# Key-value blocks of 32 by 32 in a linear-attention block, kept side by side and set onto the diagonal by ScalarE

## The chip, the core and the metric

The kernel runs on one core of a Trainium2 chip. The metric is device time in microseconds (us) of one execution. Before the change the median of three executions is 479.77 us (479.7 to 479.87). The engines are named as the profile names them: PE (TensorE), with PEld for its weight loads, DVE (VectorE), ACT (ScalarE), POOL (GpSimd) and SP (SyncE, which issues most loads).

## The reference

A transformer block with adaptive layer norm: linear attention with 32 heads of 16, then a dense Mish MLP. S is 2048, D is 512, F is 1792, and everything is fp32.

```python
def attention(h):                                  # A_ref
    q, k, v = qkv(h)                               # (1, 32, 2048, 16) each
    phi = lambda t: jnp.where(t > 0, t + 1, jnp.exp(t)) + 1e-6
    pq, pk = phi(q), phi(k)
    kv = jnp.einsum("bhsd,bhse->bhde", pk, v)      # one 16 x 16 block per head
    z = jnp.einsum("bhsd->bhd", pk)
    num = jnp.einsum("bhqd,bhde->bhqe", pq, kv)
    den = jnp.einsum("bhqd,bhd->bhq", pq, z)[..., None] + 1e-6
    return merge_heads(num / den) @ wo

sa, ca, ga, sb, cb, gb = split(silu(c) @ w_mod)    # six rows of 512
x = x + ga * attention(layernorm(x) * (1 + ca) + sa)
x = x + gb * mlp(layernorm(x) * (1 + cb) + sb)     # mlp: mish(h @ w1 + b1) @ w2
```

## The kernel before

The order of the instructions on each engine is the order in which the program is written. Pieces of side work are generators: `spawn` adds one, `spawn_idle` adds one of lower rank, and each `tick()` between two units of TensorE work takes one step of each running generator. All large SBUF tiles (128 x 512 fp32) come from one pool of 93 slots, `sb`; PSUM has four `acc`, three `h` and one `tp` bank.

Matmuls run in fp32r on halves: `split` writes a high half `...h` (ScalarE or POOL, line 82 or 84) and a low half `...l` (VectorE, line 88 or 90), and `mm3` (lines 72 to 76) issues high x high, low x high and high x low. A few small products run in plain fp32, among them the two of this case's centre: `den` (line 946, the denominators) and `kv_ps` (line 1176).

The stages in order of time, in the profiled execution:

- To about 116 us: layer norm of x in four blocks of 512 rows (each four row tiles `x_0` to `x_3`), transposes (`tp_x`, line 279), keys (`pk`, `ku`), and the Gram product `gacc` of phi(k) with the normalised x. For the early tiles the sum and the square sum come from ScalarE; `sums_eps` (line 225, then a power on POOL, line 199) turns them into 1/std `rs_x`, `sums_shift` (line 229) makes `nb_x`, and ScalarE applies both (line 208). `make_constants` builds masks on POOL at about 30 to 33 us; `bmask` (128 x 128) is one on the 16 x 16 blocks of the diagonal.
- About 116 to 126 us: the queries of the first blocks (lines 74 to 76 and 417), then `den`, then `kv_ps`: for each group g of 128 columns, the 128 x 128 block of phi(k)^T v, of which only two 64 x 64 diagonal parts are computed (j = 0, 1), summed over four row tiles `zs[k]`, `wv[k]`. VectorE writes them, times `bmask`, into the zeroed tile `kv`; `kv` is split into `kvh` and `kvl`; at 134.5 us `m_ps` (lines 74 to 76) multiplies them with wo to give `m`.
- To about 190 us: more queries, the attention output `o` (line 1001, twelve matmuls for each row tile: four groups g by three terms), the second layer norm (`rs_n`, `nb_n`, ScalarE's `n`, VectorE's 32 x 32 transposes `wide_n<-n`, line 239).
- From 190 us: the MLP as a Strassen-like scheme of seven products over quarters of w1 and w2. Sums of w1's quarters (`s`, `a`) are split early by the generator `early_rows`; the first products use `b_0h`, `b_0l` (the second layer norm) against `a_0h`, `a_0l`.

`mod_side` loads chunks of w_mod (SP) and reduces each with silu(c) on VectorE (line 175) into a column of `mc`: chunks 12 to 15 (`sb`), 16 to 19 (`cb`) and 20 to 23 (`gb`). After chunk 23, `bcast_row` turns gb's four columns into a row (`gb_ps`, TensorE; `gb_row`, ScalarE; two DMAs, POOL).

Of the kernel before, what the change touches and what calls it, by code (L numbers as in the profile page):

```python
# [25 lines left out]
def block_kernel(ctx: ExitStack, tc: tile.TileContext, x, wqkv, wo, w1, b1t, w2, c, wmodt, out):  # L26
# [11 lines left out]
    def sb(name, dt=F32, shape=(P, 512)):  # L38

        return big.tile(list(shape), dt, tag="T", name=name, bufs=SLOTS)  # L40
# [4 lines left out]
    def f32(t):  # L45
        return t.bitcast(F32)
# [97 lines left out]
    ident = cst.tile([P, P], F32, name="ident")  # L144
    make_identity(nc, ident)
    w32 = cst.tile([P, P], F32R, name="w32")
    bmask = cst.tile([P, P], F32, name="bmask")
    hmask = cst.tile([P, 4, 32], F32, name="hmask")

    kv = sb("kv")  # L150

    def make_constants():
        pool.memset(f32(w32), 1.0 / 32)
        pool.memset(kv, 0.0)

        pool.memset(bmask, 1.0)
        bm3 = bmask.rearrange("p (a r) -> p a r", r=16)
        pool.affine_select(bm3, bm3, pattern=[[-16, 8], [0, 16]], compare_op=ALU.is_ge,
                           fill=0.0, base=0, channel_multiplier=1)
        pool.affine_select(bm3, bm3, pattern=[[16, 8], [0, 16]], compare_op=ALU.is_ge,  # L160
                           fill=0.0, base=15, channel_multiplier=-1)

        pool.memset(hmask, 1.0)
        pool.affine_select(hmask, hmask, pattern=[[128, 4], [-16, 32]], compare_op=ALU.is_ge,
                           fill=0.0, base=0, channel_multiplier=1)
        pool.affine_select(hmask, hmask, pattern=[[-128, 4], [16, 32]], compare_op=ALU.is_ge,
                           fill=0.0, base=15, channel_multiplier=-1)
# [56 lines left out]
    def sums_eps(key, b, t, sums):  # L224
        dve.tensor_scalar(rs[key, b][:, t:t + 1], sums[:, 1:2], 1.0 / D, EPS, op0=ALU.mult, op1=ALU.add)  # L225
        ln_rstd(key, b, t, t + 1)
# [453 lines left out]
    apply(1, 1, act, shift=False)  # L680
    step(kpost[2])
    sums_eps("x", 1, 2, sums2)
    step(xsplit[2], kpost[2], xsplit[3])
    g_unit(0, 1)
    sums_eps("x", 1, 3, sums3)
    sums_shift("x", 1, 2, sums2)
    apply(1, 2, act, shift=False)
    step(kpost[3])
# [305 lines left out]
    def o_unit(b, t, tag="acc"):  # L994
        seeded = (b, t) in seeds
        p = seeds.pop((b, t)) if seeded else ps(tag, f"o_{b}_{t}")
        ts = slice(P * t, P * (t + 1))
        for g in range(4):
            st, mv_ = [q[:, ts] for q in qs[b, g]], ms[g]
            for i, (l, r) in enumerate(((st[0], mv_[0]), (st[0], mv_[1]), (st[1], mv_[0]))):  # L1000
                pe.matmul(p, l, r, start=not seeded and g == 0 and i == 0, stop=g == 3 and i == 2,  # L1001
                          skip_group_check=seeded)
        spawn(o_post(p, b, t, seeded))

    def later_sums(b, t):
# [146 lines left out]
    def beside_q(n):  # L1152
        if n < 4:
            load_x(1, n, "r")
        else:
            load_x(2, n - 4, "r")
        if n == 1:
            spawn(kv_side())
            spawn(wo_scale())
        if n == 4:  # L1160
            spawn(mod_side([20, 21, 22, 23, 16, 17, 18, 19], 2))
        tick()
        if n == 6:
            next(early_rows[0])
# [3 lines left out]
    kvs = {}  # L1168
    attending = attend(0, 3)
    next(attending)  # L1170
    kv_ps = ps("acc", "kv_ps")
    for g in range(4):
        for k in range(4):
            for j in range(2):
                cs = slice(P * g + 64 * j, P * g + 64 * (j + 1))
                pe.matmul(kv_ps[64 * j:64 * (j + 1), cs], wv[k][:, cs], zs[k][:, cs], start=k == 0, stop=k == 3)
    run(early_rows[0])
    for j in range(2):
        js = slice(64 * j, 64 * (j + 1))
        dve.tensor_tensor(kv.rearrange("p (g m) -> p g m", g=4)[js, :, js],  # L1180
                          kv_ps.rearrange("p (g m) -> p g m", g=4)[js, :, js],
                          bmask[js, js].unsqueeze(1).to_broadcast([64, 4, 64]), op=ALU.mult)
    kv_halves = split("kv", kv, kvs, 0)
    next(kv_halves)
    next(attending)
    run(kv_halves)
    for g in range(4):
        q_unit(2, g)
        if g == 1:
            spawn(attending)  # L1190
        if g == 2:
            spawn(attend(1, 4))
        if g == 1:
            spawn(mod_side(range(12, 16), 1))
        load_x(3, g, "r")
        if g == 2:
            for k in range(4):
                m_ps = ps("acc", f"m_ps_{k}")
                mm3(m_ps, [h[:, P * k:P * (k + 1)] for h in kvs[0]], wos[k], True, True)
                spawn(split(f"m_{k}", m_ps, ms, k))  # L1200
        tick()
    for g in range(4):
        seed_next()
        q_unit(3, g)
        tick()
        if g == 1:
            spawn_idle(early_rows[1])
            for t in range(4):
                seed_next()
                o_unit(0, t)  # L1210
                spawn(norm_first(0, t))
                if t == 1:
                    spawn(attend(2, 5, sp))
                tick()
# [471 lines left out]
```

## Time and profile before

| | |
|---|---|
| median of three executions | 479.77 us (479.7 to 479.87) |
| the profiled execution | 480.13 us, of which the span on the engines is 478.4 |
| PE busy | 471.6 us (99%) |
| DVE busy | 391.4 us (82%) |
| ACT busy | 309.3 us (65%) |
| POOL busy | 138.0 us (29%) |
| granted TensorE clock | 1.0 |
| DMA | 85.44 MB, mean 179 GB/s |

A row of the timeline reads: start in us, duration in us, engine, line of the kernel, operation, output tile<-input tiles, partitions x elements, and how many of them were grouped; in brackets the idle time of the engine before it and what ended it. For matmuls the form is contraction rows * output rows, then the moving operand. Durations of PE overlap, since matmuls are pipelined: what one costs is read from start to start. A row of the waits names the engine and the line that waited, what it waited for, and the sum, the count and the longest in us. A row of windows gives the stretch, its length, and for PE, PEld, DVE, ACT and POOL the busy time and the number of instructions, then the granted clock.

### The profile page before, as it was taken

To read this page: it belongs to the slowest core of one execution; us is meant where nothing else is said; L and a number is where in the kernel's file an instruction comes from. 1 tells how busy PE (TensorE), PEld (TensorE's weight loads), DVE (VectorE), ACT (ScalarE), POOL (GpSimd) and SP (SyncE) were. 2 spreads that over 40 slices of the span, in tenths; PEclk is the share of its full clock that TensorE was granted. 3 is DMA by queue.
4 is the path that set the end of the run, shared out by engine and by line. 5 is a ranking of instruction groups with operands and counts; after the bars stand their busy time and mean duration, and the time that the engine had idled before them with its cause. 6 is when DMAs were issued, how large, how long until landed. Compare 5 with 4: busy or idle time off the path is not lost.

```text
span 478.4 us, 7106 instructions
## 1 busy us (share of the span) xinstructions
PE 471.6 (99%) x2290; PEld 388.2 (81%) x2290; DVE 391.4 (82%) x784; ACT 309.3 (65%) x556; POOL 138.0 (29%) x235
## 2 busy tenths in 40 slices
PE   7999999999999999999999999999999999999997
PEld 6778887878887888888888888888888888888887
DVE  6989897998999889698879864899444787779992
ACT  6977559757657976588778756594256676637700
POOL 3586261100023255012225325334011101354400
PEclk9999999999999999999999999999999999999999
DMA  8913649544674356927548669999643603497974
GB/s 296 355 53 79 121 103 277 146 158 132 203 226 134 107 129 180 322 89 222 176 128 242 226 176 290 383 319 261 204 104 88 129 5 88 111 219 159 243 157 104
DMA packets 81568, 85.44 MB, mean 179 GB/s; under 512 B 23505, under 2 KB 55769, under 8 KB 81530
## 3 DMA queue, kind: packets, MB, share of 16 engines
q1 hardware_dynamic: 55176, 47.08, 33.9%
q0 software_dynamic: 24096, 37.12, 29.4%
q10 hardware_dynamic: 2258, 0.79, 0.8%
q8 instruction: 18, 0.29, 0.2%
q14 instruction: 20, 0.16, 0.1%
HBM read 55.32 MB, written 22.81 MB: 163 GB/s over the span
## 4 chain that ended last, share of the span: by engine, by line
PE 82%; DVE 7%; DMA 4%; ACT 4%; POOL 2%; issue 1%; ACTq 0%
PE p_a L1254 15%; PE o L1001 9%; PE p_s L1254 8%; PE oacc L75 5%; PE oacc L74 5%; PE oacc L76 5%; PE m L75 5%; PE m L76 5%; PE m L74 5%; PE p L1254 4%; PE pq_a L417 2%; PE pq L74 2%; PE pq L76 2%; PE pq L75 2%; DMA wm<-in_wmodt_dram 1%; PE pk L319 1%
## 5 line engine op out<-in xcount | busy, mean ns | idle before, releaser
L1259 DVE TENSOR_TENSOR cb<-p_s,u 128x512 f32<-128x512 f32 x28 | 19.2, 687 | 12.3 <-ACT u L1307 10.7
L842 POOL DMA_DIRECT2D wb<-w2d x14 | 9.8, 704 | 65.1 <-PE m L76 28.2
L1246 ACT ACTIVATE ub<-cb,b1c 128x512 f32<-128x512 f32 x28 | 20.1, 720 | 9.2 <-DVE cb L1259 8.9
L199 POOL TENSOR_TENSOR rs_n<-rs_n,half 128x1 f32<-128x1 f32 x16 | 10.1, 630 | 39.1 <-DVE rs_n L225 18.9
L1582 POOL DMA_DIRECT2D wt_m<-w2t x20 | 14.0, 702 | 25.2 <-PE m L76 16.9
L1264 ACT ACTIVATE p<-p_a 128x512 f32<-128x512 f32 x12 | 7.0, 582 | 19.8 <-PE p_a L1254 11.7
L1307 ACT ACTIVATE u<-p_a 128x512 f32<-128x512 f32 x14 | 8.4, 598 | 13.8 <-PE p_a L1254 13.6
L1221 ACT ACTIVATE u<-p,b1c 128x512 f32<-128x512 f32 x14 | 9.6, 685 | 11.5 <-PE p L1254 11.5
L1221 ACT ACTIVATE u<-p_a,b1c 128x512 f32<-128x512 f32 x14 | 9.6, 686 | 8.5 <-PE p_a L1254 8.3
L313 POOL DMA_DIRECT2D ku<-ku x10 | 8.9, 1035 | 19.6 <-DVE ku L304 19.4
L848 POOL DMA_DIRECT2D w2b<-w2d x20 | 10.6, 542 | 12.9 <-PE oacc L76 7.6
L953 POOL DMA_DIRECT2D rden_d<-rden x2 | 1.5, 737 | 42.4 <-DVE rden L951 42.4
L270 ACT ACTIVATE hf_n<-sq_n,mc 128x512 f32<-128x512 f32 x16 | 12.0, 803 | 2.4 <-DMA w2r<-in_w_dram 2.4
L304 DVE SCALAR_TENSOR_TENSOR ku<-e_k,relu_k 128x512 f32<-128x512 f32 x16 | 11.0, 685 | 0.9 <-ACT relu_k L302 0.9
L304 DVE SCALAR_TENSOR_TENSOR q<-e_q,relu_q 128x512 f32<-128x512 f32 x16 | 10.7, 690 | 1.2 <-ACT relu_q L302 1.2
L199 POOL TENSOR_TENSOR rs_x<-rs_x,half 128x1 f32<-128x1 f32 (+1 forms) x10 | 7.8, 785 | 13.1 <-DVE rs_x L194 12.2
L190 DVE BATCH_NORM_STATS2 st_x<-x 128x6 f32<-128x512 f32 x13 | 8.8, 677 | 2.9 <-DMA x<-in_x_dram 2.9
L256 POOL DMA_DIRECT2D sq_n<-wide_n x16 | 8.7, 553 | 6.8 <-DVE wide_n L239 4.7
L175 DVE SCALAR_TENSOR_TENSOR wm<-wm,sc_row 128x512 f32<-128x512 f32 x16 | 10.5, 686 | 0.0
L965 DVE SCALAR_TENSOR_TENSOR q<-q,rd 128x512 f32<-128x512 f32 x16 | 10.4, 683 | 0.1
L256 POOL DMA_DIRECT2D sq_x<-wide_x x16 | 8.9, 566 | 5.1 <-DVE wide_x L239 4.6
L301 ACT ACTIVATE e_k<-pk 128x512 f32<-128x512 f32 x16 | 9.5, 591 | 0.9 <-PE pk L322 0.9
(1634 smaller groups left out, 1862.3 us busy)
## 6 DMA issues: line engine op xcount, KB each, us to landing
wm<-in_wmodt_dram SPq DMA_DIRECT2D x24, 256.0 KB
w1p<-in_w_dram SPq DMA_DIRECT2D x24, 256.0 KB
w2b<-w2d POOLq DMA_DIRECT2D x20, 256.0 KB, 6.6
wt_m<-w2t POOLq DMA_DIRECT2D x20, 256.0 KB, 3.6
r<-in_x_dram SPq DMA_DIRECT2D x16, 256.0 KB
x<-in_x_dram SPq DMA_DIRECT2D x15, 256.0 KB
w2r<-in_w_dram SPq DMA_DIRECT2D x14, 256.0 KB
wb<-w2d POOLq DMA_DIRECT2D x14, 256.0 KB, 3.4
```

The costliest lines, as they stand in the source:

```text
L74: pe.matmul(o, st[0], mv[0], start=start, stop=False)
L75: pe.matmul(o, st[0], mv[1], start=False, stop=False)
L76: pe.matmul(o, st[1], mv[0], start=False, stop=stop)
L199: pool.tensor_tensor(y, y, half[:, lo:hi], op=ALU.pow)
L256: queues[n % len(queues)].dma_start(v[32 * m:32 * (m + 1), :, a, :], w[32 * a:32 * (a + 1), m:16:4].rearrange("p j t c -> p j (t c)"))
L304: dve.scalar_tensor_tensor(dst, e, 1.0, r, op0=ALU.min, op1=ALU.add)
L1001: pe.matmul(p, l, r, start=not seeded and g == 0 and i == 0, stop=g == 3 and i == 2, skip_group_check=seeded)
L1221: act.activation(u, p, AF.Mish, bias=b1c[:, f:f + 1])
L1246: act.activation(u, p, AF.Mish, bias=b1c[:, f:f + 1])
L1254: pe.matmul(p, st, mv, start=onto is None and c == 0 and i == 0, stop=c == 1 and i == 2, skip_group_check=onto is not None)
L1259: dve.tensor_tensor(out, p, u, op=ALU.add)
L1582: pool.dma_start(v, w2t[g][:, :, SUM[name], :])
```

## The change

1. The key-value product computes 32 x 32 diagonal blocks (j = 0 to 3) instead of 64 x 64 ones, twice as many calls, each with half the stationary and half the moving columns. The blocks lie side by side in a 128 x 128 piece of PSUM.
2. The mask `kvmask` is 128 x 32, made by a VectorE reduction of `bmask` in `make_constants`. VectorE writes `kvc` (128 x 128), it is split into `kvch` and `kvcl`, and ScalarE sets each half onto the diagonal with four copies of 32 x 4 x 32 into two tiles `kv`, zeroed by POOL during the queries.
3. `early_rows[0]`, whose last part makes the low halves of w1's first quarters, runs from the tick of the second unit of the last queries instead of right behind the product.
4. `mod_side` takes chunks 16 to 19 and 12 to 15 first; 20 to 23 (gb) come one to a tick from the last queries on.
5. The attention output's twelve matmuls are ordered by terms (high x high for all four groups, then high x low, then low x high).
6. `sums_eps` of row tile 3 of block 1 stands one place earlier.

PE around the key-value product, before (`kv_ps` stands for the product, `zs` and `wv` are its operands, a row with x2 is two calls; the pattern goes on to sixteen such rows) and then after:

```order
L946 MATMUL den_1530<-q_1_1374,hmask 32x128 x4
L946 MATMUL den_1530<-q_2_1430,hmask 32x128 x4
L946 MATMUL den_1530<-q_3_1437,hmask 32x128 x4
L1176 MATMUL kv_ps<-zs_1353,wv_958 64x64 x2
L1176 MATMUL kv_ps<-zs_1355,wv_1000 64x64 x2
L1176 MATMUL kv_ps<-zs_1357,wv_1038 64x64 x2
L1176 MATMUL kv_ps<-zs_1359,wv_1061 64x64 x2
```

```order
L946 MATMUL den_1534<-q_1_1374,hmask 32x128 x4
L946 MATMUL den_1534<-q_2_1430,hmask 32x128 x4
L946 MATMUL den_1534<-q_3_1437,hmask 32x128 x4
L1179 MATMUL kv_ps<-zs_1353,wv_958 32x32 x4
L1179 MATMUL kv_ps<-zs_1355,wv_1000 32x32 x4
L1179 MATMUL kv_ps<-zs_1357,wv_1038 32x32 x4
L1179 MATMUL kv_ps<-zs_1359,wv_1061 32x32 x4
```

Each row has become four calls of 32 x 32 where it was two of 64 x 64; `den` ahead of it already has four calls of 32 rows.

VectorE (DVE) at about 26 to 33 us, before and then after. `rs_x<-sums_x_3` is the first half of 1/std of row tile 3, `nb_x<-sums_x_3` the step that needs POOL's power of it; `xn_`, `pk_` are halves for the Gram product, `st_x` the statistics of the next block:

```order
L304 SCALAR_TENSOR_TENSOR ku_2_342<-e_k_2_343,relu_k_2_344 128x512
L225 TENSOR_SCALAR rs_x_329<-sums_x_2_376 128x1
L88 TENSOR_TENSOR xn_2l<-x_2_72,xn_2h 128x512
L90 SCALAR_TENSOR_TENSOR pk_2l<-ku_2_342,pk_2h 128x512
L225 TENSOR_SCALAR rs_x_329<-sums_x_3_387 128x1
L229 TENSOR_TENSOR nb_x_330<-sums_x_2_376,rs_x_329 128x1
L304 SCALAR_TENSOR_TENSOR ku_3_347<-e_k_3_348,relu_k_3_349 128x512
L229 TENSOR_TENSOR nb_x_330<-sums_x_3_387,rs_x_329 128x1
L88 TENSOR_TENSOR xn_3l<-x_3_77,xn_3h 128x512
L90 SCALAR_TENSOR_TENSOR pk_3l<-ku_3_347,pk_3h 128x512
L190 BN_STATS st_x_0_466<-x_0_435 128x6
L191 BN_AGGR mv_x_463<-st_x_0_466 128x2
```

```order
L304 SCALAR_TENSOR_TENSOR ku_2_341<-e_k_2_342,relu_k_2_343 128x512
L225 TENSOR_SCALAR rs_x_328<-sums_x_2_375 128x1
L225 TENSOR_SCALAR rs_x_328<-sums_x_3_386 128x1
L88 TENSOR_TENSOR xn_2l<-x_2_72,xn_2h 128x512
L90 SCALAR_TENSOR_TENSOR pk_2l<-ku_2_341,pk_2h 128x512
L229 TENSOR_TENSOR nb_x_329<-sums_x_2_375,rs_x_328 128x1
L304 SCALAR_TENSOR_TENSOR ku_3_346<-e_k_3_347,relu_k_3_348 128x512
L229 TENSOR_TENSOR nb_x_329<-sums_x_3_386,rs_x_328 128x1
L88 TENSOR_TENSOR xn_3l<-x_3_77,xn_3h 128x512
L90 SCALAR_TENSOR_TENSOR pk_3l<-ku_3_346,pk_3h 128x512
L161 TENSOR_REDUCE kvmask<-bmask 128x32
L190 BN_STATS st_x_0_466<-x_0_435 128x6
```

`rs_x<-sums_x_3` moved ahead of `xn_2l` and `pk_2l`, and `kvmask` stands between `pk_3l` and the statistics.

VectorE at about 158 to 163 us, in the second layer norm of block 0, before and then after (`wm,mc` is one chunk of w_mod; `s_1` are sums of w1's quarters):

```order
L239 STREAM_TRANSPOSE wide_n_1989<-n_0_1954 128x16x32
L1024 SCALAR_TENSOR_TENSOR nb_n_1876<-osum_1_1908,rs_n_1875 128x1
L1021 TENSOR_SCALAR rs_n_1875<-osum_2_1971 128x1
L868 TENSOR_TENSOR s_1_2000<-w1p_1_1880 128x256
L869 TENSOR_TENSOR s_1_2000<-s_1_2000,w1p_0_1879 128x256
L870 TENSOR_TENSOR s_1_2001<-w1p_0_1879,w1p_1_1880 128x256
L871 TENSOR_TENSOR s_1_2001<-w1p_0_1879,s_1_2000 128x256
L239 STREAM_TRANSPOSE wide_n_1989<-n_1_1992 128x16x32
L1024 SCALAR_TENSOR_TENSOR nb_n_1876<-osum_2_1971,rs_n_1875 128x1
L1021 TENSOR_SCALAR rs_n_1875<-osum_3_1996 128x1
L239 STREAM_TRANSPOSE wide_n_1989<-n_2_2024 128x16x32
```

```order
L175 SCALAR_TENSOR_TENSOR wm_1890,mc<-wm_1890,sc_row 128x512
L239 STREAM_TRANSPOSE wide_n_2022<-n_0_1984 128x16x32
L1023 SCALAR_TENSOR_TENSOR nb_n_1895<-osum_1_1936,rs_n_1894 128x1
L1020 TENSOR_SCALAR rs_n_1894<-osum_2_2001 128x1
L868 TENSOR_TENSOR s_1_2033<-w1p_1_1907 128x256
L869 TENSOR_TENSOR s_1_2033<-s_1_2033,w1p_0_1906 128x256
L870 TENSOR_TENSOR s_1_2034<-w1p_0_1906,w1p_1_1907 128x256
L871 TENSOR_TENSOR s_1_2034<-w1p_0_1906,s_1_2033 128x256
L175 SCALAR_TENSOR_TENSOR wm_1932,mc<-wm_1932,sc_row 128x512
L239 STREAM_TRANSPOSE wide_n_2022<-n_1_2025 128x16x32
L1023 SCALAR_TENSOR_TENSOR nb_n_1895<-osum_2_2001,rs_n_1894 128x1
L1020 TENSOR_SCALAR rs_n_1894<-osum_3_2029 128x1
```

A product of w_mod now stands ahead of each `wide_n<-n`. The four products of w_mod that stood among `q`, `qs_2l` and `qs_3l` at about 146 to 152 us are gone from there; in their place, behind the last `q`, stand `a_0l`, `s_0l`, `s_0l`, `a_0l`, which were ahead of the key-value mask.

```diff
@@ -144,21 +144,21 @@
     ident = cst.tile([P, P], F32, name="ident")
     make_identity(nc, ident)
     w32 = cst.tile([P, P], F32R, name="w32")
-    bmask = cst.tile([P, P], F32, name="bmask")
     hmask = cst.tile([P, 4, 32], F32, name="hmask")
 
-    kv = sb("kv")
+    kvmask = cst.tile([P, 32], F32, name="kvmask")
+    kv = []
 
     def make_constants():
         pool.memset(f32(w32), 1.0 / 32)
-        pool.memset(kv, 0.0)
-
+        bmask = sb("bmask", F32, (P, P))
         pool.memset(bmask, 1.0)
         bm3 = bmask.rearrange("p (a r) -> p a r", r=16)
         pool.affine_select(bm3, bm3, pattern=[[-16, 8], [0, 16]], compare_op=ALU.is_ge,
                            fill=0.0, base=0, channel_multiplier=1)
         pool.affine_select(bm3, bm3, pattern=[[16, 8], [0, 16]], compare_op=ALU.is_ge,
                            fill=0.0, base=15, channel_multiplier=-1)
+        dve.tensor_reduce(kvmask, bmask.rearrange("p (a c) -> p c a", c=32), op=ALU.add, axis=mybir.AxisListType.X)
 
         pool.memset(hmask, 1.0)
         pool.affine_select(hmask, hmask, pattern=[[128, 4], [-16, 32]], compare_op=ALU.is_ge,
@@ -680,9 +680,9 @@
     apply(1, 1, act, shift=False)
     step(kpost[2])
     sums_eps("x", 1, 2, sums2)
+    sums_eps("x", 1, 3, sums3)
     step(xsplit[2], kpost[2], xsplit[3])
     g_unit(0, 1)
-    sums_eps("x", 1, 3, sums3)
     sums_shift("x", 1, 2, sums2)
     apply(1, 2, act, shift=False)
     step(kpost[3])
@@ -995,11 +995,10 @@
         seeded = (b, t) in seeds
         p = seeds.pop((b, t)) if seeded else ps(tag, f"o_{b}_{t}")
         ts = slice(P * t, P * (t + 1))
-        for g in range(4):
-            st, mv_ = [q[:, ts] for q in qs[b, g]], ms[g]
-            for i, (l, r) in enumerate(((st[0], mv_[0]), (st[0], mv_[1]), (st[1], mv_[0]))):
-                pe.matmul(p, l, r, start=not seeded and g == 0 and i == 0, stop=g == 3 and i == 2,
-                          skip_group_check=seeded)
+        for i, (l, r) in enumerate(((0, 0), (0, 1), (1, 0))):
+            for g in range(4):
+                pe.matmul(p, qs[b, g][l][:, ts], ms[g][r], start=not seeded and g == 0 and i == 0,
+                          stop=g == 3 and i == 2, skip_group_check=seeded)
         spawn(o_post(p, b, t, seeded))
 
     def later_sums(b, t):
@@ -1158,7 +1157,11 @@
             spawn(kv_side())
             spawn(wo_scale())
         if n == 4:
-            spawn(mod_side([20, 21, 22, 23, 16, 17, 18, 19], 2))
+            for i in range(2):
+                kv.append(sb(f"kv_{i}", F32R))
+                pool.memset(f32(kv[i]), 0.0)
+        if n == 4:
+            spawn(mod_side([16, 17, 18, 19, 12, 13, 14, 15], 2))
         tick()
         if n == 6:
             next(early_rows[0])
@@ -1168,35 +1171,36 @@
     kvs = {}
     attending = attend(0, 3)
     next(attending)
-    kv_ps = ps("acc", "kv_ps")
+    kv_ps = ps("acc", "kv_ps")[:, 0:P]
     for g in range(4):
         for k in range(4):
-            for j in range(2):
-                cs = slice(P * g + 64 * j, P * g + 64 * (j + 1))
-                pe.matmul(kv_ps[64 * j:64 * (j + 1), cs], wv[k][:, cs], zs[k][:, cs], start=k == 0, stop=k == 3)
-    run(early_rows[0])
-    for j in range(2):
-        js = slice(64 * j, 64 * (j + 1))
-        dve.tensor_tensor(kv.rearrange("p (g m) -> p g m", g=4)[js, :, js],
-                          kv_ps.rearrange("p (g m) -> p g m", g=4)[js, :, js],
-                          bmask[js, js].unsqueeze(1).to_broadcast([64, 4, 64]), op=ALU.mult)
-    kv_halves = split("kv", kv, kvs, 0)
+            for j in range(4):
+                cs = slice(P * g + 32 * j, P * g + 32 * (j + 1))
+                pe.matmul(kv_ps[32 * j:32 * (j + 1), 32 * g:32 * (g + 1)], wv[k][:, cs], zs[k][:, cs],
+                          start=k == 0, stop=k == 3)
+    kvc = sb("kvc", F32, (P, P))
+    dve.tensor_tensor(kvc.rearrange("p (g m) -> p g m", g=4), kv_ps.rearrange("p (g m) -> p g m", g=4),
+                      kvmask.unsqueeze(1).to_broadcast([P, 4, 32]), op=ALU.mult)
+    kv_halves = split("kvc", kvc, kvs, 0)
     next(kv_halves)
     next(attending)
     run(kv_halves)
+    for t, tc_ in zip(kv, kvs.pop(0)):
+        for j in range(4):
+            js = slice(32 * j, 32 * (j + 1))
+            act.activation(t.rearrange("p (g m) -> p g m", g=4)[js, :, js],
+                           tc_.rearrange("p (g m) -> p g m", g=4)[js], AF.Copy)
     for g in range(4):
         q_unit(2, g)
         if g == 1:
             spawn(attending)
         if g == 2:
             spawn(attend(1, 4))
-        if g == 1:
-            spawn(mod_side(range(12, 16), 1))
         load_x(3, g, "r")
         if g == 2:
             for k in range(4):
                 m_ps = ps("acc", f"m_ps_{k}")
-                mm3(m_ps, [h[:, P * k:P * (k + 1)] for h in kvs[0]], wos[k], True, True)
+                mm3(m_ps, [h[:, P * k:P * (k + 1)] for h in kv], wos[k], True, True)
                 spawn(split(f"m_{k}", m_ps, ms, k))
         tick()
     for g in range(4):
@@ -1204,6 +1208,8 @@
         q_unit(3, g)
         tick()
         if g == 1:
+            spawn(mod_side(range(20, 24), 1))
+            spawn_idle(early_rows[0])
             spawn_idle(early_rows[1])
             for t in range(4):
                 seed_next()
```

## The prediction

> **What bounds the kernel now.** I read the page's engine shares and chain first, then TensorE's waits, then the places of the change in the timeline. The profiled execution took 480.13 us (span 478.4); the median of the shown runs is 479.77, or 0.36 less. I sum against the former and take 0.36 off at the end. About 0.2% (0.96 us) is what a measurement of this kernel can tell from no change.
>
> ```profile
> span 478.4 us, 7106 instructions
> ...
> PE 471.6 (99%) x2290; PEld 388.2 (81%) x2290; DVE 391.4 (82%) x784; ACT 309.3 (65%) x556; POOL 138.0 (29%) x235
> ...
> PE 82%; DVE 7%; DMA 4%; ACT 4%; POOL 2%; issue 1%; ACTq 0%
> ```
>
> TensorE is busy for 99% of the span and carries 82% of the chain that ends last; the rest of the chain is mostly the start and the last output. Its waits, and a stretch of 340 us:
>
> ```profile
> PE tp_x L564 <- ACT x L208: 0.6, 2, 0.4
> ...
> PE tp_late L564 <- ACT x L208: 0.4, 1, 0.4
> PE tp_x L279 <- ACT x L208: 0.3, 1, 0.3
> PE pk L319 <- ACT hT_x_2h L82: 0.3, 1, 0.3
> ```
> ```profile
> 100.00:440.00 340.00, 340.00 (x1663) 279.34 (x1663) 274.77 (x556) 226.61 (x410) 89.45 (x152) 1.00 0.63 180
> ```
>
> From 100 to 440 us TensorE is never idle (340.00 of 340.00, granted clock 1.00). So a stage there gains only what it shortens on TensorE itself, and loses whenever another engine that was just in time is not carried along by the same amount.
>
> **The key-value product on TensorE (the main term).**
>
> ```profile
> 123.20 0.81 PEld L946 LDWEIGHTS den<-q,hmask 128*32 128x32 f32 x32 [0.35 <-issue]
> 123.21 1.08 PE L946 MATMUL den<-q,hmask 128*32 128x128 f32 x32
> 124.22 1.95 PEld L1176 LDWEIGHTS kv_ps<-zs,wv 128*64 128x64 f32 x64 [0.20 <-issue]
> 124.22 2.08 PE L1176 MATMUL kv_ps<-zs,wv 128*64 128x64 f32 x64
> 126.23 0.50 PE L74 MATMUL pq<-hT_x_0h,wq_0h 128*128 128x512 f32 x1
> ```
>
> Each plain fp32 matmul stands as two passes: 32 calls for kv_ps give 64 records, 16 for den give 32. The denominators use the array as four 32-column tiles, kv_ps as two 64-column tiles. From start to start, den occupies 124.22 - 123.21 = 1.01 us and kv_ps 126.23 - 124.22 = 2.01 us. If tiles run side by side, den is 8 rounds of 128 moving columns, 1.01 / 8 / 128 = 0.99 ns a column, and kv_ps 32 rounds of 64, 2.01 / 32 / 64 = 0.98 ns a column. The new product is 64 calls of 32 columns, 128 passes in four tiles: again 32 rounds, now of 32 columns: 32 x 32 x 0.98 = 1.0 us. Gain 1.0 us; between 0.9 and 1.1, since part of the 0.20 us ahead of kv_ps may be the change of tile shape, which now falls away.
>
> The same totals allow another reading: 1.01 / 32 = 31.6 ns and 2.01 / 64 = 31.4 ns, one price per pass whatever its width. Then 128 passes take 4.0 us, a loss of 2.0. Narrow windows at the two starts tell more:
>
> ```profile
> 123.20 0.16 PEld L946 LDWEIGHTS den<-q,hmask 128*32 128x32 f32 x8 [0.35 <-issue]
> 123.21 0.32 PE L946 MATMUL den<-q,hmask 128*32 128x128 f32 x4
> 124.22 0.20 PEld L1176 LDWEIGHTS kv_ps<-zs,wv 128*64 128x64 f32 x4 [0.20 <-issue]
> 124.22 0.28 PE L1176 MATMUL kv_ps<-zs,wv 128*64 128x64 f32 x2
> ```
>
> Before 123.26 eight weight loads and four den matmuls have started, within 0.06 us: 5 ns each. So issue can run ahead in a burst. The new product needs 256 of them in 1.0 us, 4 ns each, sustained, where 128 in 2.0 us (16 ns) is all that is shown sustained. I take the columns' price because the starts stand in groups of four, not evenly spaced, and keep 2.0 us slower as the other end.
>
> The Trainium skill ("TensorE: Matmul & The Clock Gate", Part 1) says that matmuls never start closer than about 25 ns however small they are, and "TensorEngine Tiling (Array Packing)", Instruction Overhead, says not to tile a dimension that is already small. By that floor taken over all tiles the sum would be an estimated 128 x 25 = 3.2 us, 1.2 slower. The four den matmuls inside 0.06 us do not obey it across tiles; within one tile no run here shows 32 columns.
>
> **The vector and scalar work behind it.**
>
> ```profile
> 126.94 0.86 DVE L1180 TENSOR_TENSOR kv<-kv_ps,bmask 64x256 f32<-64x256 f32 x2
> 127.89 0.63 ACT L82 ACTIVATE kvh<-kv 128x512 fp32r<-128x512 f32 x1 [3.45 <-DVE kv L1180]
> 129.08 0.63 DVE L88 TENSOR_TENSOR kvl<-kv,kvh 128x512 fp32r<-128x512 f32 x1
> 134.54 0.39 PE L74 MATMUL m_ps<-wos_0h,kvh 128*128 128x512 f32 x1
> ```
>
> VectorE's mask and low half now have a quarter of the columns (0.86 + 0.63 falls to an estimated 0.5). ScalarE adds eight copies onto the diagonal; the nearest small copy (below) takes 0.25, so 2.0 us, less what the narrower high half saves. It idles 3.45 us here, more than that, and gives up the third and fourth high halves of w1 to about 151 as well. The m products need kv at 134.54, one us earlier now, about 133.5; kv is ready by about 128.5. Zero on TensorE. If ScalarE were late, its e_q would follow, not the m products.
>
> ```profile
> L474 ACT ACTIVATE gb_row<-gb_ps x1: 252/252/252, 146.8 to 146.8; 4x128 f32<-4x128 f32 x1
> ...
> L781 DVE TENSOR_TENSOR w2g<-w2r,gb_bc x28: 384/420/424, 207.1 to 283.6; 128x256 f32<-128x256 f32 x28
> ```
>
> gb's transpose, its row copy and its two DMAs on POOL's queue move from 144-155 to about 176-190; the first user starts at 207.1, so this is free. Two memsets of kv on POOL replace one. SP only exchanges the order of w_mod's chunks, with the last four behind x's rows. The output products keep their 12 matmuls each; by terms, they want all high halves within three matmuls' time and the low halves later. Both are costed at nothing: the high halves come from ScalarE before the low ones from VectorE, which were the closer.
>
> **The start of the kernel.**
>
> ```profile
> 28.42 0.15 DVE L225 TENSOR_SCALAR rs_x<-sums_x 128x1 f32<-128x1 f32 x1
> ...
> 30.03 0.55 DVE L229 TENSOR_TENSOR nb_x<-sums_x,rs_x 128x1 f32<-128x1 f32 x1 [0.44 <-POOL rs_x L199]
> ...
> 31.70 0.68 DVE L190 BATCH_NORM_STATS2 st_x<-x 128x6 f32<-128x512 f32 x1
> ...
> 37.27 0.68 DVE L88 TENSOR_TENSOR hT_x_3l<-hf_x,hT_x_3h 128x512 fp32r<-128x512 f32 x1
> ```
> ```profile
> 30.64 0.52 POOL L154 MEMSET kv<- 128x512 f32 x1
> ...
> 32.06 0.34 POOL L160 TENSOR_SCALAR_AFFINE_SELECT bmask<-bmask 128x128 f32<-128x128 f32 x1
> ```
> ```profile
> 30.67 0.81 ACT L208 ACTIVATE x<-x,nb_x,rs_x 128x512 f32<-128x512 f32 x1 [0.83 <-DVE nb_x L229]
> 31.54 1.64 PE L279 MATMUL tp_x<-ident,x 128*128 128x128 f32 x13 [0.33 <-ACT x L208]
> 38.24 0.39 PE L322 MATMUL pk<-wk_3h,hT_x_3l 128*128 128x512 f32 x1
> ```
> ```profile
> L750 DVE TENSOR_REDUCE zh<-zbc_sb x1: 681/681/681, 113.6 to 113.6; 128x32 f32<-128x512 f32 x1
> ```
>
> With the variance of row tile 3 taken two instructions earlier, POOL's power is done before VectorE asks: the 0.44 us wait at 30.03 goes, and with it up to 0.33 us of TensorE's wait at 31.54. Against it stands the new kvmask reduction on VectorE, behind pk_3l and ahead of the statistics of block 1. It waits for POOL's second mask select, which ends at 32.06 + 0.34 = 32.40 now and 0.52 (no memset) to 0.96 (the power earlier too) sooner then, at 31.4 to 31.9. VectorE reaches the reduction at 31.70 - 0.44 = 31.3, so it waits 0.1 to 0.6 us, and then reduces: between a small operation's 0.15 and the 0.68 of the only other reduction, which reads four times as much; I take 0.3. The statistics then start at 31.7 to 32.2 instead of 31.70, and hT_x_3l ends at 38.0 to 38.45 instead of 37.95. TensorE wants it at 38.24, or at 37.9 if it used the earlier transposes in full. Net +0.1 us, between -0.33 (the mask hidden) and +0.45 (the mask late and its reduction slow).
>
> **What is given back at 190 us.**
>
> ```profile
> 160.32 0.70 DVE L239 STREAM_TRANSPOSE wide_n<-n 128x512 f32<-128x512 f32 x1
> ...
> 162.41 0.71 DVE L239 STREAM_TRANSPOSE wide_n<-n 128x512 f32<-128x512 f32 x1 [1.07 <-ACT n L208]
> ...
> 165.64 0.71 DVE L239 STREAM_TRANSPOSE wide_n<-n 128x512 f32<-128x512 f32 x1 [0.37 <-ACT n L208]
> ```
> ```profile
> 124.80 0.69 DVE L88 TENSOR_TENSOR a_0l<-w1p,a_0h 128x512 fp32r<-128x512 f32 x1
> 146.12 0.69 DVE L175 SCALAR_TENSOR_TENSOR wm<-wm,sc_row 128x512 f32<-128x512 f32 x1
> 189.28 0.68 DVE L88 TENSOR_TENSOR b_0l<-hf_n,b_0h 128x512 fp32r<-128x512 f32 x1
> 190.30 0.39 PE L75 MATMUL p_a<-b_0l,a_0h 128*128 128x512 f32 x1
> ```
>
> The MLP's first product needs b_0l, ready at 189.28 + 0.68 = 189.96, 0.34 us before TensorE reads it at 190.30. TensorE now comes 0.9 earlier (1.0 less the start's 0.1), VectorE must follow. The four low halves of w1 (from 124.80 to the mask at 126.94, 2.1 us) leave for 148 to 152, just where four products of w_mod (about 0.6 each) stood; those move to 158-165, one ahead of each wide_n. There 1.07 + 0.37 us of idle can take two of them; the other two (1.2 us) eat VectorE's lead, which at 158 is about 1.0 (TensorE's, which feeds it) to 2.0 (with the 1.0 saved on kv). That leaves 0 to 0.8, say 0.4, ahead; TensorE then waits 0.9 - 0.4 - 0.34 = 0.16, about 0.2 us, between 0 and 0.56.
>
> **Sum.** -1.0 + 0.1 + 0.2 = -0.7 us: a profiled execution of about 479.4, and a median of 479.77 - 0.7 = 479.1 us. That is within what cannot be told from no change.
>
> **Rivals.**
> - Issue bounds the 32 by 32 product (slower). Place: kv_ps alone. It decides once a pass costs over 2.0 / 128 = 16 ns; at 31.4 it takes 4.0 us, so 479.77 + 2.0 + 0.1 = 481.9; at half of the excess 480.9. For it: two groups at one price per pass, no sustained faster issue shown. Against: the bursts.
> - Nothing is given back (faster). VectorE's idle before wide_n and the kv savings carry it along, and the earlier transposes come through: -1.0 to -1.1 and -0.1 to -0.33: 478.3 to 478.7. For it: the 1.07 and 0.37 us of idle; against: the 0.34 us of room at 190.30.
> - The mask's wait or the later w_mod products take back the whole gain: +0.45 at 38 us and +0.56 at 190 against -1.0: 479.8, no change at all.
>
> **How the numbers follow.** The sum as worked out has 0.42; nothing given back 0.26; the whole gain taken back 0.12; issue-bound 0.20, most of it over the bound. The likeliest case reaches from 478.9 to 479.5, all but its lower edge within 0.2%. Faster: 0.26 and 0.06 of the likeliest's edge, 0.32. Slower: 0.18 of the issue case and 0.02 of the third, 0.20. The same: 0.48. The range 478.3 to 481.3 takes in the faster rival whole and the issue case up to 27 ns a pass, and leaves out some 0.1 beyond.
>
> **What would show it.** In the profile after: kv_ps from start to the next product about 1.0 us (2.0 or more: issue); den to kv_ps without the 0.20 us gap; a kvmask with 0.1 to 0.6 us of waiting for POOL ahead of it, and hT_x_3l ending at 38.0 to 38.45; wide_n without the 1.07 us of idle; a TensorE wait of about 0.2 us at b_0l near 189.4. The forecast is wrong if kv_ps is not shortened, if the m products wait for the copies onto the diagonal, or if an o product waits for its high halves.

## The result: 482.86 us, 0.65% slower, and the profile after

The changed kernel takes 482.86 us (median of six, 482.19 to 483.67) against 479.74 for the kernel before (479.53 to 480.15): a ratio of 1.0065, 95% interval 1.0054 to 1.0076. The forecast was 479.1 with a range to 481.3, so both the value and its range were wrong: 3.1 us were lost where 0.7 were to be won.

The page, TensorE's waits and the key-value product, after:

```profile
span 481.2 us, 7247 instructions
...
PE 79%; DVE 9%; ACT 4%; issue 4%; POOL 2%; DMA 2%; DVEq 0%; ACTq 0%; POOLq 0%
```
```profile
PE o L1000 <- ACT qs_2h L82: 0.9, 1, 0.9
PE den L946 <- DVE q L304: 0.9, 1, 0.9
...
PE pk L322 <- DVE hT_x_0l L88: 0.7, 1, 0.7
```
```profile
123.68 1.08 PE L946 MATMUL den<-q,hmask 128*32 128x128 f32 x32
124.58 1.28 PE L1179 MATMUL kv_ps<-zs,wv 128*32 128x32 f32 x128
125.79 0.50 PE L74 MATMUL pq<-hT_x_0h,wq_0h 128*128 128x512 f32 x1
125.95 0.29 DVE L1182 TENSOR_TENSOR kvc<-kv_ps,kvmask 128x128 f32<-128x128 f32 x1 [0.59 <-PE kv_ps L1179]
```

The product did what it was to do. From den's start to the first query product it is 125.79 - 123.68 = 2.11 us, where it was 126.23 - 123.21 = 3.02: 0.91 us less, 0.80 of it in `kv_ps` and 0.11 ahead of it. Three waits of TensorE that were not there before cost several times as much. The two large ones go back to one instruction on VectorE (rows of the timeline, by engine):

```profile
159.10 2.69 SPq L957 DMA_DIRECT2D rd<-rden_d  x4
161.88 0.41 SPq L103 DMA_DIRECT2D wm<-in_wmodt_dram  x1
```
```profile
169.06 0.69 DVE L175 SCALAR_TENSOR_TENSOR wm<-wm,sc_row 128x512 f32<-128x512 f32 x1 [3.59 <-DMA wm<-in_wmodt_dram]
...
169.67 0.71 DVE L239 STREAM_TRANSPOSE wide_n<-n 128x512 f32<-128x512 f32 x1
170.30 0.65 DVE L304 SCALAR_TENSOR_TENSOR q<-e_q,relu_q 128x512 f32<-128x512 f32 x1
```
```profile
171.01 0.42 PE L946 MATMUL den<-q,hmask 128*32 128x128 f32 x8 [0.86 <-DVE q L304]
189.97 0.50 PE L1000 MATMUL o<-m_2h,qs_2h 128*128 128x512 f32 x1 [0.91 <-ACT qs_2h L82]
```

w_mod's last chunk (23) is issued on SP at 161.88, behind the four loads of rd, and lands 7.2 us later. Its product on VectorE waits 3.59 us for it, until 169.06, and since VectorE works in program order, the last wide_n, a query and all that follows wait too. TensorE misses the query at 171 and, at the end of VectorE's chain, a high half at 190. Read from start to start this costs it 1.1 us at 171, 0.5 at 180 (a low half) and 1.6 from 188 to 191.

The table follows TensorE's lead over the profiled execution of the kernel before, taken instruction by instruction: the start of one matmul less the start of the same matmul before (negative is earlier). That execution (480.13 us) was itself slow at its start: every other kernel here is 0.3 to 0.8 us earlier at 30 us, in code that hardly differs up to there. So it is the steps from column to column that count.

| us in the profile before | 30 | 40 | 122 | 127 | 153 | 169 | 189.5 | end |
|---|---|---|---|---|---|---|---|---|
| changed kernel | -0.45 | +0.44 | +0.48 | -0.44 | -0.61 | -0.61 | +2.66 | +2.76 |
| e1_load_ahead | -0.44 | +0.42 | +0.48 | -0.46 | -0.61 | -0.61 | -0.40 | -0.34 |
| e2_mask_late | -0.68 | -0.49 | -0.10 | -1.02 | -1.17 | -1.17 | +1.45 | +1.50 |
| e3_both | -0.82 | -0.63 | -0.27 | -1.18 | -1.34 | -1.34 | -1.12 | -1.02 |
| e4_kv_alone | -0.43 | -0.41 | -0.31 | -1.23 | -0.31 | -0.31 | -0.31 | -0.31 |
| e6_mask_at_kv | -0.36 | -0.17 | -0.13 | -1.05 | -1.20 | -1.20 | -0.50 | -0.44 |
| e11 (e6 again) | -0.41 | -0.20 | -0.12 | -1.03 | -1.20 | -1.20 | -0.95 | -0.89 |
| e12_loads_sooner | -0.30 | -0.07 | -0.04 | -0.95 | -1.13 | -1.13 | -0.89 | -0.86 |

The changed kernel loses 0.89 at the start (30 to 40 us), wins 0.92 at the product, 0.15 where gb's transpose left (143 us), and loses 3.27 between 169 and 189.5. From there to the end nothing changes.

### The profile page after: what moved, and what is told of

Its sections match the earlier page's. It is cut to its first block, busy times and chain, and to the rows that moved or that the text cites. A ratio compares the mean times of both kernels' runs of the same rounds, so it can differ in the third digit from the quotient of the medians.

```text
span 481.2 us, 7247 instructions
## 1 busy us (share of the span) xinstructions
PE 471.9 (98%) x2354; PEld 386.9 (80%) x2354; DVE 389.8 (81%) x784; ACT 311.7 (65%) x564; POOL 138.8 (29%) x236
## 4 chain that ended last, share of the span: by engine, by line
PE 79%; DVE 9%; ACT 4%; issue 4%; POOL 2%; DMA 2%; DVEq 0%; ACTq 0%; POOLq 0%
PE p_a L1260 15%; PE p_s L1260 8%; PE o L1000 6%; PE oacc L75 5%; PE oacc L74 5%; PE oacc L76 5%; PE m L75 5%; PE m L74 5%; PE m L76 5%; PE p L1260 4%; PE pq_a L417 2%; PE pk L319 2%; PE pq L74 2%; PE pq L75 2%; PE pq L76 2%
## 5 line engine op out<-in xcount | busy, mean ns | idle before, releaser
L208 ACT ACTIVATE x<-x,nb_x,rs_x 128x512 f32<-128x512 f32 x9 | 7.0, 808 | 5.4 <-DVE nb_x L203 4.6
```

## The experiments

### e1 to e4: the load's place, the mask's place, both, and the product alone

e1_load_ahead, in the changed kernel (`mod_side` gets a list of chunks that it loads one tick sooner):

```diff
-    def mod_side(order, per, lag=3):
+    def mod_side(order, per, lag=3, ahead=()):
...
-            for i in steps[n] if n < len(steps) else ():
-                load_wmod(i)
+            for i in steps[n] if n < len(steps) else ():
+                if i not in ahead:
+                    load_wmod(i)
+            if n == 2:
+                for i in ahead:
+                    load_wmod(i)
...
-            spawn(mod_side(range(20, 24), 1))
+            spawn(mod_side(range(20, 24), 1, 3, (23,)))
```

> The changed kernel, with the load of w_mod's last chunk (23) issued on SP one tick earlier, ahead of the four loads of rd instead of behind them; the order on every other engine stays. Theory Q (place in SP's queue): the changed kernel loses its time where VectorE waits 3.59 us for that chunk at 165.5 to 169.1 us; with the load ahead the wait is gone, TensorE no longer waits for a query at 171 nor for high halves at 190, and the median falls from 482.86 by 2.7 to 3.6 to 479.3 to 480.2. Rival D (the four products of w_mod are too much for VectorE in this stretch wherever their data are): 2.4 us of work stay, and the median falls by at most 1 us, to 481.9 or more. Rival T (the transfers are slow there, since x's rows, w1 and rd share the DMA engines): the chunk lands late again, 482.4 to 482.9.

Measured: 479.86 us, ratio to the kernel before 1.0003 (0.9994 to 1.0012); before in the same comparison 479.67. The last three loads of w_mod now stand ahead of rd's, chunk 23's at 146.2 instead of 161.9 us:

```profile
141.42 5.12 SPq L103 DMA_DIRECT2D wm<-in_wmodt_dram  x3
...
159.08 2.64 SPq L961 DMA_DIRECT2D rd<-rden_d  x4
```

Moving one load by one tick gives back 3.0 us. The four products are all still there, so it was not their number; and the same transfer, issued earlier, is in time, so it was its place in SP's queue. Theory Q held, its two rivals fell.

e2_mask_late and e3_both (the latter with e1's edit):

```diff
     def make_constants():
...
-        dve.tensor_reduce(kvmask, bmask.rearrange("p (a c) -> p c a", c=32), op=ALU.add, axis=mybir.AxisListType.X)
...
     g_unit(0, 3)
     spawn(ln_begin(2))
     spawn(ln_turn(2, (0, 1), ()))
     tick()
+    dve.tensor_reduce(kvmask, bmask.rearrange("p (a c) -> p c a", c=32), op=ALU.add, axis=mybir.AxisListType.X)
```

> The changed kernel, with the reduction to kvmask moved on VectorE from ahead of the statistics of block 2 to behind the low halves and transposes that follow them (about 41 us). Theory: TensorE's wait for hT_x_0l (0.65 us at 36.7) goes, TensorE is 0.4 to 0.8 us earlier from 37 us to the end, and the median is 482.1 to 482.5. Rival: the loss at 190 us is set by a transfer whose time does not move with TensorE, and takes back what the start gives: 482.8 to 482.9.

> Both edits: last w_mod chunk loaded ahead of rd, and the reduction to kvmask late. If the two losses are separate and the product's gain of 0.9 us is real: the start at least as early as before, 478.5 to 479.2, faster than before by 0.5 to 1.2 us. If the room of 0.34 us at the MLP's first product binds: 479.0 to 479.5. Rival D (VectorE overloaded by the moved w_mod products): 481 or more.

Measured: e2 482.21 us, 1.0052 (1.004 to 1.0065); e3 479.74 us, 1.0001 (0.9992 to 1.001). At 40 us both are 0.9 to 1.1 ahead of the changed kernel, but 0.4 of it goes at 82 us, where TensorE waits for ScalarE's hT_x_2h: 0.8 us over its usual spacing, where it was 0.44. e2's median is 0.65 us under that of the changed kernel, though the intervals of their ratios overlap; e3's median gains only 0.1 against e1, though its profiled execution (479.11 us) is 1.0 under that of before. Its other executions run from 479.28 to 481.1, which the next runs take up.

e4_kv_alone is the kernel before with the new product, mask (late) and copies; nothing else is moved:

```diff
-            for j in range(2):
-                cs = slice(P * g + 64 * j, P * g + 64 * (j + 1))
+            for j in range(4):
+                cs = slice(P * g + 32 * j, P * g + 32 * (j + 1))
...
     run(early_rows[0])
...
+    kvc = sb("kvc", F32, (P, P))
```

> The kernel before with only the 32 by 32 product, its mask (reduced late), the copies onto the diagonal and the two memsets; w1's low halves, the order of w_mod, the output products and the variance of row tile 3 stay as before. If the product alone carries the gain and the moves add nothing: 478.6 to 479.1. If TensorE, 0.9 us earlier, runs into VectorE's low halves at 190 us (0.34 us of room) because the low halves of w1 still stand ahead of the key-value mask: 479.3 to 479.7. If the copies on ScalarE delay the m products: over 479.8.

Measured: 479.79 us, 1.0003 (0.9994 to 1.0012). The product is 0.92 faster here too (-0.31 to -1.23), and all of it is gone at 148 us. That is neither of the places that were named. VectorE waits for the rd transfers, then TensorE for VectorE's low half:

```profile
138.38 1.29 DVE L966 SCALAR_TENSOR_TENSOR q<-q,rd 128x512 f32<-128x512 f32 x2 [1.18 <-DMA rd<-rden_d]
```
```profile
PE o L1002 <- DVE qs_2l L88: 0.6, 1, 0.6
```

This run changes more than the product, though. With other tiles in the slots of `sb`, a load of w_mod on SP that waits for the m products until 135.19 in the kernel before is released by `kvcl` and starts at 128.34 here, while the denominators are on their way through memory. The load in the kernel before and in e4, then the window from 130 to 132 us in the kernel before and in e4 (the last two numbers are the busy share of the DMA engines and GB/s):

```profile
135.19 0.33 SPq L103 DMA_DIRECT2D wm<-in_wmodt_dram  x1
```
```profile
128.34 0.33 SPq L103 DMA_DIRECT2D wm<-in_wmodt_dram  x1
```
```profile
130.00:132.00 2.00, 2.00 (x10) 1.68 (x9) 2.00 (x6) 1.57 (x4) 0.23 (x1) 1.00 0.14 34
```
```profile
130.00:132.00 2.00, 2.00 (x11) 1.65 (x10) 2.00 (x7) 2.00 (x4) 0.00 (x0) 1.00 0.98 326
```

So the product alone, with these earlier loads that come with it, is worth nothing on this kernel. The moves are what can carry its gain past 148 us, and one of them was badly placed.

### e5 to e8: what remains of the gain, and what carries it

> The kernel of e3_both once more, for another execution's trace: its profiled execution took 479.11 us and its other ten 479.28 to 481.1. If the spread is a wait that comes in some executions, this trace, where it is a slower one, has a TensorE wait that the other lacks, at one place after 126 us. If the executions differ before 126 us alone (the start's loads), TensorE's lead from 127 us on is the same in both.

Measured: 479.79 us, 0.9999 (0.999 to 1.0008); the profiled execution 479.52. TensorE's lead over e3's trace differs by 0.4 us at the start and is then parallel to the end; neither trace has a wait that the other lacks. This run did not show what makes the slower executions.

e6_mask_at_kv: e3 with the reduction beside its only user.

```diff
+    bmask = cst.tile([P, P], F32, name="bmask")
...
+    kvmask = sb("kvmask", F32, (P, 32))
+    dve.tensor_reduce(kvmask, bmask.rearrange("p (a c) -> p c a", c=32), op=ALU.add, axis=mybir.AxisListType.X)
     kvc = sb("kvc", F32, (P, P))
```

> e3_both with the reduction to kvmask right ahead of kvc on VectorE, where VectorE waits 0.59 us for kv_ps anyway; bmask keeps its place from before, and kvmask takes a slot there. In e3_both the reduction at 41 us left VectorE 0.3 us later, and TensorE's wait for hT_x_2h at 82 us grew from 0.44 to 0.80. If the reduction is what grew it: 0.3 us less than e3_both, 479.3 to 479.5. If that wait grows because TensorE comes earlier there while ScalarE and VectorE do not: no change, 479.6 to 479.8.

Measured: 479.24 us against 479.84, 0.999 (0.9982 to 0.9999). The excess at 82 us is back from 0.80 to 0.47, so it was the reduction (0.34 us) in VectorE's chain at 41 us that grew it. The median is 0.6 us under the kernel before, and the interval just leaves out no change (that of e11, the same kernel again, does not). In its trace TensorE's lead falls from 1.20 to 0.50 between 169 and 189.5.

e7_kv64 is e6 with the kernel before's product and mask, and the copies left out; e8_o_by_g is e6 with the loops of the output product exchanged:

```diff
-        for i, (l, r) in enumerate(((0, 0), (0, 1), (1, 0))):
-            for g in range(4):
+        for g in range(4):
+            for i, (l, r) in enumerate(((0, 0), (0, 1), (1, 0))):
```

> e6_mask_at_kv with the key-value product of the kernel before (64 by 64 blocks, mask on the full tile, halves of 512 columns, no copies onto the diagonal); every move stays. If the product's 0.9 us reaches the end: 0.9 us slower than e6_mask_at_kv. If TensorE's lead is taken back by a wait behind it (the MLP's first product at 190 us, with 0.34 us of room): slower by 0 to 0.4 us only.

> e6_mask_at_kv with the twelve matmuls of an output product in the order of before, by groups. In e4_kv_alone TensorE waited 0.6 us for the low half qs_2l at 148 us. If the order by terms is what avoids that: 0.3 to 0.9 us slower than e6_mask_at_kv. If moving w1's low halves and gb's chunks already left VectorE early enough (by 2 us there): the same as e6_mask_at_kv within 0.2 us.

Measured: e7 480.85 us, 1.002 (1.0011 to 1.0029), 1.6 slower than e6 and 1.0 slower than the kernel before: without the product the moves cost time. With the moves in place all of the product's gain reaches the end, and more: between the two traces TensorE's lead differs by 0.96 at 127 us and by 1.2 at the end, where VectorE is 1.2 us later too (kvc takes 0.29 us instead of 0.86, and its low half less). The other 0.4 of the medians' 1.6 is that e6's profiled execution (479.68 us) was longer than its median. e8 479.25 us, 0.9991 (0.9982 to 1.0): the order by terms makes no difference here.

e8's profiled execution (480.35 us) was the longest of its ten, and shows where such an execution loses its time. Rows of e8 on VectorE and TensorE:

```profile
136.40 0.69 DVE L967 SCALAR_TENSOR_TENSOR q<-q,rd 128x512 f32<-128x512 f32 x1 [0.69 <-DMA rd<-rden_d]
137.57 0.69 DVE L967 SCALAR_TENSOR_TENSOR q<-q,rd 128x512 f32<-128x512 f32 x1 [0.47 <-DMA rd<-rden_d]
...
154.62 0.69 DVE L967 SCALAR_TENSOR_TENSOR q<-q,rd 128x512 f32<-128x512 f32 x1 [0.63 <-DMA rd<-rden_d]
```
```profile
190.13 0.50 PE L75 MATMUL p_a<-b_0l,a_0h 128*128 128x512 f32 x1 [0.39 <-DVE b_0l L88]
```

VectorE waited 1.8 us for rd here, in e6's own trace 1.1 and in e3's 0.5. The waits at 136 to 138 us are mostly taken back: at 145 us VectorE is 0.9 later than in e3, at 152 only 0.2 (in e6 0.75, then 0.15). But they send the next denominators out later as well, and at 154 us VectorE waits for their rd. From there to 190 us it stays 0.6 (e6) and 0.9 (e8) later than in e3, and TensorE meets that at 187 to 190: in e8 at the product and the low half that the prediction named, in e6 at an output product ahead of it.

### e9 to e12: VectorE's load, or the transfers

e9 puts gb's chunks where the kernel before had its last four (and needs e1's edit no longer):

```diff
         if g == 2:
             spawn(attend(1, 4))
+        if g == 1:
+            spawn(mod_side(range(20, 24), 1))
...
-            spawn(mod_side(range(20, 24), 1, 3, (23,)))
```

e10 puts w1's low halves back as well, and e11 is e6 again:

```diff
+    run(early_rows[0])
     kvmask = sb("kvmask", F32, (P, 32))
...
-            spawn_idle(early_rows[0])
             spawn_idle(early_rows[1])
```

> e6_mask_at_kv with w_mod's last four chunks (gb) loaded and reduced where the kernel before has its last four (from the second unit of the third queries, on VectorE at 146 to 152 us), instead of one ahead of each wide_n. In e6_mask_at_kv VectorE is 2.0 us ahead of the kernel before at 152 us and only level with it at 169 us, while TensorE is 1.2 ahead; 1.2 us of that goes on the first two of these products at 158 to 161. If their place is what takes VectorE's lead: VectorE keeps 0.3 to 0.7 us at 169, TensorE waits less at 187 to 190, and the median is 0.3 to 0.5 us under e6_mask_at_kv's, 478.7 to 479.0. If VectorE is held at 153 us by waits that come anyway (for ScalarE's qs_0h and for rd): the same as e6_mask_at_kv, 479.2.

> e9_gb_as_before with w1's first low halves back ahead of the key-value mask too, so that of the changed kernel only the 32 by 32 product, its mask reduced beside it, the order by terms and the earlier variance of row tile 3 are left. kvc then stands behind 2.1 us of low halves on VectorE, as the mask did before. If VectorE's lead from 127 us on comes from moving the low halves: it is gone, TensorE waits at 148 us as in e4_kv_alone (0.6 us) unless the order by terms hides it, and the median is 479.4 to 479.9. If not: as e9_gb_as_before.

> e6_mask_at_kv once more, on the same chip as the two others, to compare with them: 479.1 to 479.4, 0.4 to 0.7 us under the kernel before.

Measured, against 479.86: e9 481.29 us (479.91 to 484.02), 1.0037 (1.002 to 1.0054); e10 480.57 us, 1.0014 (1.0005 to 1.0023); e11 479.4 us (479.2 to 481.0), 0.9995 (0.9987 to 1.0003). e9 was expected at 478.7 to 479.2 and missed by two us, in the other direction; e10, expected at 479.4 to 479.9 or as e9, lies between the two and is slower than the kernel before; e11 is at the upper edge of its range. The waits, of e9 and then of e10:

```profile
136.46 0.69 DVE L963 SCALAR_TENSOR_TENSOR q<-q,rd 128x512 f32<-128x512 f32 x1 [0.36 <-DMA rd<-rden_d]
138.41 0.69 DVE L963 SCALAR_TENSOR_TENSOR q<-q,rd 128x512 f32<-128x512 f32 x1 [1.25 <-DMA rd<-rden_d]
```
```profile
140.02 1.30 DVE L963 SCALAR_TENSOR_TENSOR q<-q,rd 128x512 f32<-128x512 f32 x2 [2.25 <-DMA rd<-rden_d]
```

Against e6's trace VectorE in e9 is 1.0 us later at 138 us, behind the wait for rd. The four products, which now stand among the low halves of w1, make that 2.5 at 150, and 1.4 is left from 168 us to the first product of the MLP. So the wait for rd is the larger part of what stays; the executions of e9 above 483 us have no trace.

e10 and the kernel before send the denominators off at nearly the same time (129.23 and 129.47), and rd is issued at 133.29 and 132.76. From 128 to 134 us the DMA engines are 97% busy or more in e10, and 23% or less in the kernel before; the first rd lands 6.7 us after its issue in e10, 3.9 in the kernel before.

The theory that formed then: the denominators go to memory and come back as rd at 127 to 137 us, SP's loads of x's rows and of w_mod run beside them, and these loads hold them up. e12_loads_sooner tests it from the other side: e6 with eight loads one tick sooner and their products where they were.

```diff
-        if n == 4:
-            spawn(mod_side([16, 17, 18, 19, 12, 13, 14, 15], 2))
+        if n == 3:
+            spawn(mod_side([16, 17, 18, 19, 12, 13, 14, 15], 2, 4))
```

> e6_mask_at_kv with w_mod's chunks 16 to 19 and 12 to 15 loaded one tick sooner on SP (some 2 us, the last by about 122 instead of 124 us), their products on VectorE where they were. In two executions of e6_mask_at_kv VectorE waited 0.97 and 0.24 us at 136 us for the rd transfers, which follow the denominators' round trip through memory at 127 to 132 us; in e9 and e10, where more of SP's loads ran at 128 to 133 us, it waited 1.6 and 2.25. If it is these loads that hold the round trip up: the wait at 136 us is under 0.3 us, VectorE keeps 0.3 to 0.7 us more at 169 us, and the median is 0.2 to 0.5 us under e6_mask_at_kv's, 478.8 to 479.2. If the loads wait for slots that come free no sooner, or x's rows are what holds the round trip up: 479.2 to 479.5 as before.

Measured: 479.09 us against 479.87, 0.9984 (0.9975 to 0.9993), and eleven executions within 479.0 to 479.34, where e6 and e11 reached 480.3 and 481.0. VectorE no longer waits for rd at 136 us at all. The windows from 130 to 132 us, of e9, of e12 and of e6 (length, busy time and count of PE, PEld, DVE, ACT, POOL, clock, DMA share, GB/s), and the issues on POOL, of e9, of e12 and of e6:

```profile
130.00:132.00 2.00, 2.00 (x10) 1.65 (x10) 1.97 (x8) 2.00 (x5) 0.00 (x0) 1.00 0.97 340
```
```profile
130.00:132.00 2.00, 2.00 (x11) 1.65 (x10) 1.97 (x7) 2.00 (x5) 1.09 (x2) 1.00 0.50 136
```
```profile
130.00:132.00 2.00, 2.00 (x11) 1.65 (x10) 1.97 (x7) 2.00 (x5) 0.00 (x0) 1.00 0.05 17
```
```profile
127.18 0.77 POOL L951 DMA_DIRECT2D rden_d<-rden  x1 [14.99 <-DVE kvcl L88]
132.12 2.42 POOL L955 DMA_DIRECT2D rd<-rden_d  x4 [4.18 <-DMA rden_d<-rden]
```
```profile
127.30 0.77 POOL L955 DMA_DIRECT2D rden_d<-rden  x1 [14.32 <-DVE kvcl L88]
130.91 2.42 POOL L959 DMA_DIRECT2D rd<-rden_d  x4 [2.85 <-ACT e_q L299]
```
```profile
127.21 0.77 POOL L955 DMA_DIRECT2D rden_d<-rden  x1 [14.99 <-DVE kvcl L88]
132.51 2.42 POOL L959 DMA_DIRECT2D rd<-rden_d  x4 [4.54 <-DMA rden_d<-rden]
```

The denominators leave at the same time, 127.2 to 127.3. In e9, with the DMA engines 97% busy, POOL waits 4.18 us for them to land and issues rd at 132.12; in e12, with 50%, they have landed by 130.91. But the busy share of this window does not settle it: in e6 it is 5%, and POOL waits 4.54 us and issues rd at 132.51. So e10 and e12 bear the theory out as a whole, and what it is in the loads that holds the denominators up is not shown.

This is the fastest version here, 0.78 us under the kernel before. Its interval overlaps e6's, and in the profiled executions e11 (479.26) and e12 (479.27) are equal: what e12 avoids is the long executions. As e6, e11 and e12 ran on three chips, some of the narrower spread may be the chip's (the kernel before reached from 479.59 to 480.26 beside e12, from 479.59 to 480.55 beside e6 and from 479.77 to 480.96 beside e11).

## Why the prediction was wrong, by its own steps

- **The product on TensorE**: right. Forecast -1.0, measured -0.91 (2.11 us instead of 3.02, kv_ps itself 1.21 where 1.0 was forecast). 128 passes in 1.21 us are 9.5 ns each, where it would have been 31 by the price per pass; the rival of the issue bound fell. The Trainium skill's floor of about 25 ns ("TensorE: Matmul & The Clock Gate", Part 1), taken over all tiles, does not hold in this trace: its passes come faster.
- **Vector and scalar work behind it**: right. kvc took 0.29 us, and the m products did not wait.
- **"SP only exchanges the order of w_mod's chunks, with the last four behind x's rows"**, which was given no cost: this is the step that failed, and it is 3.0 of the 3.8 us between the forecast and the result. The last four chunks did not stand only behind x's rows: the program's order on SP, which could be read before the run, has the last one behind rd's loads.

```text
L103 DMA wm_1932<-in_wmodt_dram 128x512
L103 DMA wm_1981<-in_wmodt_dram 128x512
L953 DMA rden_d_1991<-rden_1988 4x32x128
L957 DMA rd_0_1993<-rden_d_1991 128x1x512
L957 DMA rd_1_1995<-rden_d_1991 128x1x512
L957 DMA rd_2_1997<-rden_d_1991 128x1x512
L957 DMA rd_3_1999<-rden_d_1991 128x1x512
L103 DMA wm_2019<-in_wmodt_dram 128x512
```

  The prediction followed the chunks' products on VectorE (2.4 us) and never their data. It cost 3.0 us (482.86 to 479.86 in e1). Most of the other 0.8 is the start.
- **The start**: mechanism right, size off. Forecast +0.1 with a bound of +0.45. The mask's wait was 0.65 and its reduction 0.39, and TensorE waited 0.65 for hT_x_0l, not for hT_x_3l:

```profile
30.95 0.69 DVE L90 SCALAR_TENSOR_TENSOR pk_3l<-ku,pk_3h 128x512 fp32r<-128x512 f32 x1 [0.51 <-POOL pk_3h L84]
32.29 0.39 DVE L161 TENSOR_REDUCE kvmask<-bmask 128x32 f32<-128x128 f32 x1 [0.65 <-POOL bmask L159]
```
```profile
36.74 0.50 PE L322 MATMUL pk<-wk_0h,hT_x_0l 128*128 128x512 f32 x1 [0.65 <-DVE hT_x_0l L88]
```

  The wait of 0.44 at nb_x went, as forecast. But the earlier first half of 1/std now waits 0.95 us for ScalarE's sums, a wait that the prediction did not have:

```profile
27.33 0.15 DVE L225 TENSOR_SCALAR rs_x<-sums_x 128x1 f32<-128x1 f32 x1 [0.95 <-ACT scrap_x L221]
```

  So ku and the rest of VectorE's work come no earlier, POOL idles 0.68 us before pk_3h at 29.83, pk_3l waits 0.51 for that, and the masks end hardly earlier than before (32.26 instead of 32.40). Between 30 and 40 us the changed kernel loses 0.89; e6, with the earlier variance and no reduction there, 0.19; e4, with neither, 0.02. So the reduction, with its wait, cost about 0.7, and the earlier variance won nothing: the 0.3 us that TensorE gains at the transposes (30 to 35 us) goes again at the same low halves.
- **Given back at 190 us**: the size of 0.2 is met where rd is in time (e1 0.21, e3 0.22, e12 0.24 from 169 to 189.5). The mechanism is borne out in part: the MLP's first product with b_0l starts 0.10 to 0.14 us behind b_0l there, where the room was 0.34, but no wait of it is long enough to be listed, and some of the loss lies in steps at 176 and 188 us ahead of it. A wait at b_0l is listed in e8 alone (0.39). The upper bound of 0.56 was too small: 0.70 in e6, where VectorE also comes late from rd's landing, which the prediction did not look at.
- **The rivals**: none held this mechanism. "The mask's wait or the later w_mod products take back the whole gain" named the right chunks but priced VectorE's work only, and stopped at 479.8.

## What to carry to other kernels

When a step is moved, follow its data as well as its work: write down what stands ahead of its load in the queue that issues it, and when the last of those can start; an engine that works in order then waits for that load with everything behind it. A faster stage has no worth of its own: the product's 0.91 us was nothing in the kernel before (e4) and 1.6 among the moves (e6 against e7), which without it cost 1.0. All together gained 0.8 once the reduction stood in an idle moment and the large loads came sooner (e12). Where executions of one kernel spread by a us or more, look for a transfer that lands just in time.

## What the runs showed of the hardware that was not expected

- Four column tiles of 32 by 32 sustained one fp32 pass in 9.5 ns, with their weight loads (128 of each in 1.21 us).
- One 256 KB load, queued behind four broadcast loads of rd, landed 7.2 us after its issue. The trace has the landing of one other load of this group, issued at 115.6, and that took 2.7.
- The busy share of the DMA engines did not tell how long a small transfer takes to land: with the denominators issued at 127.2, POOL could issue rd at 132.5 in e6, with a share of 5% from 130 to 132 us, and at 132.1 in e9, with 97%.
- The spread of the executions was widest where loads ran beside the round trip (479.91 to 484.02 in e9) and narrowest where they came sooner (479.0 to 479.34 in e12); that the loads alone make it is not shown.
